# Loads of the next couples moved behind batch 0's block turns, and the next batch's z turned within a couple

## The chip, the cores and the metric

One core of one Trainium2 chip. The metric is the time on the device of one execution, in microseconds. Each comparison runs the kernel before and the changed one in turn on the same chip. The runs carry a state; ratios are the mean time of one kernel's fast runs over that of the other's fast runs of the same rounds, so they are not quite the ratio of the medians that I also quote. For a program on one core a run counts as slow when it is over 1.5% above the fastest of the same kernel. The kernel before spreads so widely (949 to 976 us over all calls) that this rule drops some of its longest runs; where it matters I say so. "Clock" is the clock that the chip granted to TensorE (the matmul engine) as a share of full speed; a "wait" is idle time of an engine before an instruction; a DMA "lands" when its data has arrived.

## The reference, cut to what matters

```
# u, v: (8, 3072, 256), z: (8, 3072, 64)
scores = (1.0 / S) * np.matmul(z, z.transpose(0, 2, 1))
attn = np.maximum(scores, 0.0) ** 2
x = (u * np.matmul(attn, v)).reshape(8 * 3072, 256)
return np.maximum(x @ w1, x @ w2) @ w_out
```

The scores are symmetric, so the kernel computes a block of 512 x 512 of the upper triangle once and gets its mirror by a transposing DMA, which I call a block turn.

## The kernel before

A batch has 6 groups of 512 rows; two groups are a couple. Batch 0 runs its first four groups in a plain stage, then its last couple; batches 1 to 7 run three couples each, and behind each couple a stage for the feed-forward part of the couple before. All turns (blocks, z and u) are issued in order by SyncE; all loads and stores by GpSimd, apart from batch 0's z, which SyncE loads.

```python
def mirror(b, g, blk):                      # a block turn: 128 x 2048 bf16, 512 KB
    t = Block(turned=True)
    nc.sync.dma_start_transpose(
        t.ap.rearrange("p (k r) -> p k r", r=P), A[b, g, blk].ap)
    ...
def load_z(b, piece, held=False):           # piece: a third of a batch's z
    zn[b, piece] = zpool.tile([P, 2 * G, dqk], bf16, name="zn")
    ...
    nc.gpsimd.dma_start(out=zn[b, piece], in_=...)      # fp32 to bf16
def turn_z(b, piece):
    t = zpool.tile([P, 2 * G, 2, dqk], bf16, name="zd")
    for h in range(2):
        nc.vector.tensor_copy(t[:, :, h, :], zn[b, piece])
    nc.sync.dma_start_transpose(zT[:, ds(z_at(b, piece * 2 * G), 2 * G), :], ...)
# ... load_v, load_u, turn_u alike
# plain stage, group i = 3:
if (i, n) == (3, 14):
    load_z(1, 2, held=True)
if (i, n) == (3, 18):
    load_v(1, 2, held=True)
if (i, n) in ((3, 12), (3, 20)):
    load_u(0, 4 + (n == 20))
# ...
# in a couple: at a step of TensorE an event can be run
for half, (name, w, blk, j) in enumerate(pair):
    ...
    if (s, half) in marks:                  # a half-done sum goes to the other half of the rows
        relay = nc.gpsimd.nop()             # TensorE waits for this relay some steps later
```

The relay matters below: GpSimd passes on a semaphore for TensorE between its own DMA issues, in program order.

## Time and profile before

| | kernel before |
|---|---|
| median, range | 965.23 us, 961.29 to 974.57 (3 runs) |
| TensorE busy | 910.9 of 961.9 us |
| longest waits of TensorE | 15.9 us for a block turn (once), 9.9 us for turns of z (five times) |
| DMA queues over the span | turns 60.7%, loads and stores 29.7% of 16 engines |

The lines, and what is read from them, are in the prediction.

### The profile page before, as it was taken

The page shows a single profiled execution, that of the slowest core. Times are in us where ns is not written, and L with a number is a line of the kernel's source. Part 1 is how long each engine was busy: PE and PEld are TensorE (multiplying, and loading weights), DVE is VectorE, ACT ScalarE, POOL GpSimd, SP SyncE. Part 2 cuts the span into 40 slices and gives each one's busy share as a digit, 9 for nine tenths or more (in the row PEclk, how much of TensorE's full clock was granted, in tenths as well). Part 3 has the DMA queues.
Part 4 walks back from the last instruction along what each step waited for, and adds up shares of the span by engine and source line. Part 5 has one row for each costly group of instructions (what it writes and reads, how often), then busy time and mean ns, then how long its engine had stood idle before and what let it go on. Part 6 is the DMA issues. An engine that isn't in the chain of part 4 may idle for free. (4 is left out here: it accounts for less than half of the span.)

```text
span 961.9 us, 19245 instructions
## 1 busy us (share of the span) xinstructions
PE 910.9 (95%) x7490; PEld 509.9 (53%) x7538; DVE 726.1 (75%) x1098; ACT 601.1 (62%) x1185; POOL 109.4 (11%) x207
## 2 busy tenths in 40 slices
PE   8994899999999999999999999999799999999995
PEld 3453454654655545555546545555365554555553
DVE  6770388796997789887997979978599788995620
ACT  6792677666675666666666666666566666664253
POOL 3110001101101101001111011011010110100000
PEclk9998899999999999999999999999999999999998
DMA  9999999999799997999989996989969899796211
GB/s 186 158 185 155 149 177 151 161 160 171 145 184 142 158 189 126 165 175 172 165 135 182 164 164 138 179 151 165 130 142 167 172 160 168 131 176 115 68 44 45
DMA packets 382509, 145.99 MB, mean 152 GB/s; under 512 B 361937, under 2 KB 365905, under 8 KB 382417
## 3 DMA queue, kind: packets, MB, share of 16 engines
q1 hardware_dynamic: 359328, 90.09, 60.7%
q0 software_dynamic: 23088, 54.67, 29.7%
q8 instruction: 59, 0.97, 0.4%
q14 instruction: 34, 0.27, 0.1%
HBM read 59.77 MB, written 25.17 MB: 88 GB/s over the span
## 5 line engine op out<-in xcount | busy, mean ns | idle before, releaser
L848 PE MATMUL acc<-blk,v_sb 64*128 64x512 bf16 x2208 | 454.4, 379 | 15.9 <-DMA blk<-blk 15.9
L221 ACT ACTIVATE r_sb<-s_ps 128x512 bf16<-128x512 f32 (+3 forms) x664 | 332.0, 556 | 148.6 <-PE s_ps L208 115.1
L848 PE MATMUL acc<-blk,vt 64*128 64x512 bf16 x1512 | 365.4, 377 | 0.0
L848 PEld LDWEIGHTS <-v_sb 64*128 64x128 bf16 x2208 | 180.3, 95 | 156.0 <-issue 23.5
L229 DVE TENSOR_TENSOR blk<-r_sb 128x1024 bf16<-128x1024 bf16 x251 | 168.8, 689 | 86.0 <-ACT r_sb L221 84.8
L454 PE MATMUL o_ps<-w_out_sb,g_sb 128*128 128x256 bf16 x1536 | 207.6, 273 | 7.3 <-ACT g_sb L438 5.0
L438 ACT ACTIVATE g_sb<-d_ps 128x512 bf16<-128x512 f32 x384 | 193.3, 630 | 27.6 <-PE acc L848 17.3
L848 PEld LDWEIGHTS <-vt 64*128 64x128 bf16 x1512 | 139.6, 94 | 62.6
L454 PEld LDWEIGHTS <-g_sb 128*128 128x128 bf16 x1536 | 150.0, 98 | 37.8 <-ACT g_sb L438 19.3
L431 PE MATMUL d_ps<-xT,w_sb 128*128 128x512 bf16 x720 | 167.5, 379 | 2.6 <-issue 0.2
L462 ACT COPY o_sb<-o_ps 128x512 f32<-128x512 f32 x96 | 56.2, 585 | 154.3 <-PE o_ps L454 111.9
L208 PE MATMUL s_ps<-zT 64*128 64x512 bf16 (+3 forms) x672 | 128.7, 359 | 10.8 <-DMA zT<-zd 9.9
L752 DVE TENSOR_TENSOR h_sb<-h_sb,acc 128x512 f32<-128x512 f32 x168 | 109.5, 683 | 28.4 <-ACT h_sb L756 18.6
L431 PEld LDWEIGHTS <-w_sb 128*128 128x128 bf16 x768 | 73.2, 98 | 89.6 <-issue 9.8
L463 POOL DMA_DIRECT2D out_dram<-o_sb x96 | 52.3, 545 | 562.2 <-ACT o_sb L462 562.2
L227 DVE TENSOR_TENSOR blk<-r_sb 128x512 bf16<-128x512 bf16 (+3 forms) x170 | 49.0, 323 | 56.9 <-ACT r_sb L221 55.8
L767 DVE TENSOR_TENSOR blk<-blk,blk 128x2048 bf16<-128x2048 bf16 x63 | 76.7, 1219 | 10.4 <-PE acc L848 10.4
L325 DVE TENSOR_TENSOR blk<-blk,blk 128x2048 bf16<-128x2048 bf16 x63 | 76.8, 1219 | 4.8 <-DMA blk<-blk 4.8
L329 DVE TENSOR_TENSOR blk<-blk,blk 128x2048 bf16<-128x2048 bf16 x63 | 77.2, 1225 | 2.1
L446 PE MATMUL o_ps<-W2o_sb,xT 128*128 128x256 bf16 x384 | 73.3, 273 | 0.0
L333 DVE TENSOR_TENSOR blk<-blk,blk 128x2048 bf16<-128x2048 bf16 x63 | 73.3, 1219 | 0.0
L208 PEld LDWEIGHTS <-zT 64*128 64x128 bf16 x672 | 36.9, 94 | 50.8 <-DMA zT<-zd 12.9
(51 smaller groups left out, 329.5 us busy)
## 6 DMA issues: line engine op xcount, KB each, us to landing
out_dram<-o_sb POOLq DMA_DIRECT2D x96, 256.0 KB, 3.1
un<-in_u_dram POOLq DMA_DIRECT2D x48, 256.0 KB, 6.7
v_sb<-in_v_dram POOLq DMA_DIRECT2D x21, 512.0 KB, 7.2
blk<-blk SPq DMA_TRANSPOSE x246, 5.7
zn<-in_z_dram POOLq DMA_DIRECT2D x21, 128.0 KB, 4.2
v_sb<-in_v_dram POOLq DMA_DIRECT2D x6, 256.0 KB, 8.0
blk<-in_moe_w_dram POOLq DMA_DIRECT2D x2, 512.0 KB, 6.4
uT<-un SPq DMA_TRANSPOSE x48, 4.8
```

Source lines behind the costliest of these rows:

```text
L208: nc.tensor.matmul(s_ps[h][:, lo[h] :], zT[rows, z_at(b, blk * G + tiles[h]), :], zT[rows, q + lo[h] // P : q + G, :].rearrange("p t c -> ...
L221: nc.scalar.activation(o, s, AF.Relu)
L229: nc.vector.tensor_mul(a[:, k : k + 2, :], r, r)
L325: nc.vector.tensor_add(*alike(f["S1"], f["A21"], f["A22"]))
L329: nc.vector.tensor_sub(*alike(f["S2"], f["S1"], f["A11"]))
L333: nc.vector.tensor_sub(*alike(f["S3"], f["A11"], f["A21"]))
L431: nc.tensor.matmul(d_ps, w15_sb[:, kc, ts(nb, P)], xT[:, kc, :], start=(kc == 0), stop=(kc == KD - 1),)
L438: nc.scalar.activation(g_sb[:, nb, :], d_ps, AF.Relu)
L454: nc.tensor.matmul(o_ps[:, t, :], g_sb[:, nb, ts(t0 + t, P)], w_out_sb[:, nb, :], start=False, stop=(nb == KF - 1),)
L752: nc.vector.tensor_add(out, a, b_)
L767: nc.vector.tensor_sub(f["A12"].ap, f["A12"].ap, f["S2"].ap)
L848: mm = nc.tensor.matmul(a.out(acc[name]), w()[rows], a.moving(rows, j), start=name not in opened, stop=left[name] == 0,)
```

## The change

It means to leave the DMA queues to the block turns while these have a backlog, and to have z turned long before the scores want it.

```diff
@@ plain stage, group 3
-                if (i, n) == (3, 14):
-                    load_z(1, 2, held=True)
-                if (i, n) == (3, 18):
-                    load_v(1, 2, held=True)
-                if (i, n) in ((3, 12), (3, 20)):
-                    load_u(0, 4 + (n == 20))
@@
-        second(PLAIN // 2 - 2, tasks + [lambda: turn_z(1, 2)])
+        second(PLAIN // 2 - 2, tasks)
@@ events of couple c of batch b (before: z loaded at 20, 30 and 20)
+                        (8, load_z, b + 1, 0),
+                        (14, load_z, b + 1, 1),
+                        (44, turn_z, b + 1, 0),
+                        (58, turn_z, b + 1, 1),
+                    ],
+                    [(8, load_z, b + 1, 2), (44, turn_z, b + 1, 2), (45, load_v, b + 1, 2)],
+                    [(10, load_v, b + 1, 1)],
@@ batch 0's last couple
+            if not b:
+                plan = [
+                    (2, load_z, 1, 2),
+                    (10, load_v, 1, 2),
+                    (20, turn_z, 1, 2),
+                    (24, load_u, 0, 4),
+                    (28, load_u, 0, 5),
+                    (40, load_v, 1, 1),
+                    (60, turn_u, 0, 4),
+                    (66, turn_u, 0, 5),
+                    (80, load_u, 1, 0),
+                    (88, load_u, 1, 1),
+                ]
@@ the stage behind a couple
-                if b and b + 1 < B and c < 2:
-                    tasks += [
-                        lambda piece=piece: turn_z(b + 1, piece) for piece in ((0, 1), (2,))[c]
-                    ]
```

(Cut: the same events written as a list instead of lambdas.)

More of the change, by code (lines that the diff above doesn't have):

```diff
@@ L808 @@
                 events[len(steps)] = [after_plain]
-            for n, do in (
-                (1, lambda: turn_u(b, q1)),
-                (4, lambda: turn_u(b, q2)),
-            ):
-                events.setdefault(n, []).append(do)
-            if i + 1 < len(couples):
-                later_b, later_c = couples[i + 1]
-                for n, g in ((36, 2 * later_c), (44, 2 * later_c + 1)):
-                    events.setdefault(n, []).append(lambda g=g: load_u(later_b, g))
-            for n, do in ():
-                events.setdefault(n, []).append(do)
-            if b + 1 < B:
-                for n, do in (
-                    ((20, lambda: load_z(b + 1, 0)), (30, lambda: load_z(b + 1, 1))),
-                    ((20, lambda: load_z(b + 1, 2)), (45, lambda: load_v(b + 1, 2))),
-                    ((10, lambda: load_v(b + 1, 1)),),
-                )[c]:
-                    if b or c == 2:
-                        events.setdefault(n, []).append(do)
+            plan = [(1, turn_u, b, q1), (4, turn_u, b, q2)]
+            if i + 1 < len(couples):
+                nb, nc_ = couples[i + 1]
+                plan += [(36, load_u, nb, 2 * nc_), (44, load_u, nb, 2 * nc_ + 1)]
+            if b + 1 < B:
+                plan += (
+                    [
+                        (8, load_z, b + 1, 0),
[5 more added lines that the diff above has]
+                    [(10, load_v, b + 1, 1)],
+                )[c]
+            if not b:
[11 more added lines that the diff above has]
+                ]
+            for n, do, *what in plan:
+                events.setdefault(n, []).append(lambda do=do, what=what: do(*what))
             asked = 0
```

## The prediction

> **What bounds the kernel now.** I read the page first, then the list of waits of TensorE, then the timeline around its longest wait, then the DMA queues of two stretches before that wait, and last the windows with their clocks.
>
> ```profile
> span 961.9 us, 19245 instructions
> PE 910.9 (95%) x7490; PEld 509.9 (53%) x7538; DVE 726.1 (75%) x1098; ACT 601.1 (62%) x1185; POOL 109.4 (11%) x207
> PE   8994899999999999999999999999799999999995
> PEclk9998899999999999999999999999999999999998
> ```
>
> TensorE is the bound: 910.9 of 961.9 us busy. About 51 us of the span is idle time of TensorE, and only that, with work done at a reduced clock, can be won without removing matmuls. The slices show two holes: slices 3 and 4 (digits 4 and 8) and slice 28 (digit 7). The list of waits of TensorE names them (engine, tile and line, what it waited for: us in total, times, longest):
>
> ```profile
> PE acc L848 <- DMA blk<-blk: 15.9, 1, 15.9
> PE s_ps L208 <- DMA zT<-zd: 9.9, 5, 5.2
> PE o_ps L454 <- ACT g_sb L438: 5.0, 28, 0.2
> ```
>
> One wait of 15.9 us is for a turned score block; five waits of 9.9 us in sum are for a turned z. Next the timeline of the issuing queues (SPq issues the turns, POOL the loads) and of TensorE:
>
> ```profile
> 50.22 0.54 POOL L180 DMA_DIRECT2D un<-in_u_dram  x1
> 57.78 34.75 SPq L257 DMA_TRANSPOSE blk<-blk  x7
> 65.09 0.53 POOL L132 DMA_DIRECT2D zn<-in_z_dram  x1 [14.33 <-DVE zn L131]
> 66.54 0.53 POOL L154 DMA_DIRECT2D v_sb<-in_v_dram  x1 [0.92 <-DVE v_sb L153]
> 67.06 0.54 POOL L180 DMA_DIRECT2D un<-in_u_dram  x1
> 92.64 2.73 SPq L140 DMA_TRANSPOSE zT<-zd  x1
> 95.47 4.52 SPq L257 DMA_TRANSPOSE blk<-blk  x2
> 99.98 1.01 PE L848 MATMUL acc<-blk,v_sb 64*128 64x512 bf16 x3 [15.88 <-DMA blk<-blk]
> ```
>
> Batch 0's last couple starts at 83.7 us and stops after one matmul: its first pair of steps needs block (5,4), the turned (4,5), and that is the last of batch 0's 15 turns in the queue. It was issued at 95.47 and landed at 99.94. From the trace's semaphore times and the program's wait values, what that turn reads was written by 63 us and its destination was free by 43; none of the turns issued from 57.8 to 97.6 waited for data. The queue itself was late. The DMA queues for 56 to 68 us, then for 68 to 86 us (packets, MB, share of 16 engines):
>
> ```profile
> q1 hardware_dynamic: 9355, 2.35, 115.5%
> q0 software_dynamic: 17, 0.02, 4.4%
> ```
> ```profile
> q1 hardware_dynamic: 2583, 0.65, 87.6%
> q0 software_dynamic: 501, 1.18, 39.7%
> ```
>
> Alone, the turns (q1) moved 2.35 MB in 12 us. Beside the loads of z, v and u (q0) they moved 0.65 MB in 18 us. A turn's packet took 1.155 x 16 x 12 us / 9355 = 24 ns in the first stretch and 0.876 x 16 x 18 us / 2583 = 98 ns in the second. One block landed every 2.4 us from 63.0 to 68.0; the next took 22 us. The windows add the clock (stretch, its length, busy us of PE, PEld, DVE, ACT, POOL with counts, then granted clock, DMA share, GB/s):
>
> ```profile
> 86.00:100.00 14.00, 0.02 (x2) 0.02 (x3) 0.00 (x0) 1.17 (x2) 1.08 (x2) 0.53 1.07 226
> 100.00:104.00 4.00, 4.00 (x22) 2.29 (x23) 1.26 (x4) 1.54 (x4) 0.00 (x0) 0.52 1.10 210
> 679.00:684.20 5.20, 0.07 (x2) 0.00 (x0) 1.22 (x2) 0.48 (x1) 0.00 (x0) 0.99 1.02 140
> 684.20:687.60 3.40, 3.38 (x18) 1.22 (x20) 1.46 (x2) 1.08 (x2) 1.07 (x2) 0.51 1.19 243
> ```
>
> After both long idle stretches TensorE works about 3.4 to 4 us at half clock.
>
> **What the Trainium skill says.** "DMA: Bandwidth & Descriptors", section "Issuing engines are not separate DMA queues", says that DMAs issued by sync and by gpsimd end on the same 16 DMA engines and interleave. The 24 against 98 ns agree. The same page, "Queues, rings and completion order", says that an engine goes round its queue rows a packet at a time. The trace has packets of 256 bytes for turns and of 1 to 4 KB for loads, so a turn should lose more than an equal share; 0.65 MB of turns against 1.18 MB of the others agrees in direction. "TensorE: Matmul & The Clock Gate", section "What's actually happening", gives half clock after an idle window of about 3.4 us and full clock after about as long of sustained work. The trace agrees: half clock to 103.86 after the first wait and to 687.54 after the one of 5.2 us.
>
> **The change, part by part.**
>
> (a) Removed from the plain stage: u of group 4 (issued 50.22), z piece 2 (65.09), v piece 2 (66.54) and u of group 5 (67.06), 256 + 128 + 512 + 256 = 1152 KB as landed. The turns keep their program order up to the one needed and the next. Without the loads, after the landing at 67.99 there remain four blocks, one z turn and the needed block. At 2.4 us a block and half for z that is 5.5 x 2.4 = 13.2 us: landing at 81.2. Group 4's load at 50.22 went beside a turn whose issue took 4.2 us against about 2.1 undisturbed, so the queue should be about 2 us earlier still: 79. Two stores (74.3 and 76.5) stay beside them; in 88 to 94 us two such stores cost about 1 us. So I expect landing near 80 to 82, before the 83.7 when it is needed. Gain: 15.9 us.
>
> (b) No idle stretch, no half clock: 99.98 to 103.86 at half costs 3.88 / 2 = 1.9 us. Gain 1.9.
>
> (c) z of the next batch. All five waits for zT fall in the third couple of a batch and are for piece 2, which before is turned at the end of the stage behind the second couple. Its turn is issued as the third couple starts, beside the load of v and two stores; in four of the five cases it took 8.6 to 14.3 us to land (4.4 is the median of all z turns), in the fifth it landed in 3.3 but was issued 7.6 us into the couple, behind a block turn. The change turns it at step 44 of the second couple's 84, with its load at step 8. A couple of this kind takes 21 us and the stage behind it 16.3 (653.3 to 669.6), so the turn is issued about 10 + 16 = 26 us earlier, and even 14.3 us to landing is covered. Gain 9.9 us (0.6 + 1.5 + 1.5 + 5.2 + 1.2), and at 684.22 to 687.54 another 3.3 / 2 = 1.7 us of half clock. The count of copies and turns stays, so VectorE has the same work in other places (two copies of 286 ns each).
>
> (d) Added to batch 0's last couple: the 1152 KB, together with v of piece 1, which moves from step 10 to 40. The loads of u for batch 1 move to steps 80 and 88. The first of these waits for the turn of group 4's u, and GpSimd also relays half-done matmuls in this couple; the last relays that TensorE waits for are at steps 83 and 87, wanted at 88 and 92. The couple takes 26.8 - 1.9 = 24.9 us for 96 steps, so step 80 is at +20.7 and step 88 at +22.8. Group 4's load is issued at +6 and should land by +13 to +16 (in this couple's traffic of before, v took 7.2 us, u 6.0 and 8.2); its turn follows in 5 to 8 us. It is just in time. Likewise z piece 2 is loaded at step 2, turned at step 20 (+5.2) and wanted by scores at step 58 (+15.1): with 4.4 us median and 10 us under load it fits, without much room. For these two I give back 2.5 us.
>
> Sum: 15.9 + 1.9 + 9.9 + 1.7 - 2.5 = 26.9 us. From the median of 965.2: 938.3 us. I say 938.
>
> **Rivals.** First, the stall moves: the loads collide with the turns inside the last couple, the z or u turns land 10 to 16 us after issue, and TensorE waits 3 to 8 us there or at the start of batch 1. For it: loads of v and u beside turns made a landing of 22 us once. Against it: that was with a backlog of turns, while in this couple the turns are held back by their own data and landings stayed under 10 us before. Time then 942 to 948. Second, the slow stretch from 68 to 86 is not due to the loads: from 76 to 82 us q0 moved little, yet turns stayed slow, and two stores were in flight. Then the needed block lands late all the same, perhaps half the wait stays, and the time is about 947. Against it: v and u were still unfinished until 81.7 and 83.3, and two stores at 88 to 91 left the turns near their pace. Third, z turns inside a couple delay the mirrored blocks behind them on the in-order queue, and VectorE waits: 2 to 4 us. Against it: VectorE waited for blocks only 4.8 us in all, and it is 75% busy.
>
> **Range and chances.** With everything won and nothing given back it is 965.2 - 29.4 = 936; a quicker before run takes some us off this (its three runs lie 961.3 to 974.6). With the first or second rival it is 942 to 951. So 931 to 951 holds it 8 times in 10. Two per cent is 945.9, a gain of 19.3: it needs all of (a), (b) and a little, or half of (a) with all of (c). Faster 0.84, same 0.15, slower 0.01.
>
> **What would show it.** The waits of TensorE: the one for blk<-blk gone or under 2 us, those for zT<-zd gone; clock at 1.00 from 80 to 110 and near 684 minus the gain. The needed block's turn landing before 84 and turns at about 24 ns a packet from 56 to 80. A new line of waits for zT or for GpSimd between 84 and 110 us would be rival one; a block wait of 5 us or more with no loads beside it, rival two. I am wrong if the stalls vanish and the span does not fall with them.

## The result, and the profile after

The changed kernel took 939.57 us (936.79 to 942.12, 4 runs) beside 969.32 us (961.29 to 974.57) of the kernel before: ratio 0.970, interval 0.962 to 0.978. The page of the changed kernel, its span and two rows of the 40 slices:

```profile
span 939.1 us, 19291 instructions
PE   9999889999999999999999999999999999999995
PEclk9999999999999999999999999999999999999998
```

Slices are counted from 0. Slices 3 and 28, at 4 and 7 before, are at 9. Slice 4 is at 8 as before, and slice 5 went from 9 to 8: there the new waits lie. TensorE's waits from batch 0's last couple on (engine, tile and line, what it waited for: us in total, times, longest; those of 0.2 us and less are left out):

```profile
PE acc L853 <- POOLq L862: 2.1, 1, 2.1
PE acc L853 <- DVE blk L329: 1.6, 1, 1.6
PE s_ps L208 <- ACT o_sb L462: 1.2, 1, 1.2
PE s_ps L208 <- DMA zT<-zd: 0.6, 1, 0.6
```

No wait for a block turn is left, and of 9.9 us for turned z only 0.6, in another place. Four small new waits, 5.5 us in sum, all lie between 98 and 133 us. The queue of turns in the changed kernel, where the needed block is the first of the two turns in the second line:

```profile
72.89 1.79 SPq L140 DMA_TRANSPOSE zT<-zd  x1
74.78 6.96 SPq L257 DMA_TRANSPOSE blk<-blk  x2
```

It was issued at 74.78 in place of 95.47 and landed at 81.88. The last couple began at 83.0, 1.1 us later, and did not wait. The DMA queues of 68 to 86 us, to compare with the same stretch in the prediction (q1 holds the turns, q0 the loads and stores; packets, MB, share):

```profile
q1 hardware_dynamic: 10865, 2.73, 93.8%
q0 software_dynamic: 320, 1.05, 17.9%
```

The turns moved 2.73 MB in these 18 us in place of 0.65. A packet of a turn took 0.938 x 16 x 18 us / 10865 = 25 ns in place of 98. The 1.05 MB of q0 are mostly the four stores. Two of them (73.59 and 75.77) ran beside the turns up to the needed one. These turns landed 6.5 to 7.1 us after issue, where the four before them took 4.6 to 4.7, and from 73 to 82 us turns and stores together moved 205 GB/s, beside 214 for turns alone from 68 to 72.9 us. So two stores beside turns cost a few us, and are not what made the slow stretch. The windows of the changed kernel (length, busy us of PE, PEld, DVE, ACT, POOL, then granted clock, DMA share, GB/s):

```profile
86.00:100.00 14.00, 13.37 (x126) 6.14 (x124) 7.11 (x14) 11.23 (x22) 1.96 (x4) 1.00 1.04 141
128.80:132.20 3.40, 1.22 (x10) 0.41 (x7) 3.33 (x4) 0.65 (x2) 0.54 (x1) 1.00 1.26 139
132.20:135.70 3.50, 2.92 (x15) 1.16 (x16) 3.50 (x4) 2.49 (x5) 1.08 (x2) 0.51 1.23 286
```

Where TensorE stood idle before (86 to 100), it works at full clock. After the waits of 1.6 and 1.2 us the clock was at half from 132.25 to 135.66 us, and TensorE was busy for 2.9 us of that.

The sum over the two traces: 15.9 + 1.9 + 9.9 + 1.7 = 29.4 us went, 5.5 us of waits and 2.9 / 2 = 1.4 us of half clock came, which leaves 22.5; the spans differ by 961.9 - 939.1 = 22.8. The medians of the timed runs differ by more, 29.7. That is the first sign that one trace of the kernel before is not all of it.

### The profile page after: what moved, and what is told of

It reads as the page before. It is cut to its first block, busy times and chain, and to the rows that moved or that the text cites. A ratio compares the mean times of both kernels' runs of the same rounds, so it can differ in the third digit from the quotient of the medians.

```text
span 939.1 us, 19291 instructions
## 1 busy us (share of the span) xinstructions
PE 912.3 (97%) x7538; PEld 516.2 (55%) x7538; DVE 722.4 (77%) x1096; ACT 599.0 (64%) x1185; POOL 110.2 (12%) x207
## 5 line engine op out<-in xcount | busy, mean ns | idle before, releaser
L853 PEld LDWEIGHTS <-v_sb 64*128 64x128 bf16 x2208 | 176.7, 94 | 138.0 <-issue 9.8
L431 PE MATMUL d_ps<-xT,w_sb 128*128 128x512 bf16 x768 | 173.9, 379 | 0.0
L746 DVE TENSOR_TENSOR h_sb<-h_sb,acc 128x512 f32<-128x512 f32 x168 | 109.5, 683 | 26.5 <-ACT h_sb L750 18.8
L415 DVE SCALAR_TENSOR_TENSOR xT<-h_sb,uT 128x512 bf16<-128x512 f32 x96 | 59.9, 684 | 0.0
```

The source lines that it names most:

```text
L431: nc.tensor.matmul(d_ps, w15_sb[:, kc, ts(nb, P)], xT[:, kc, :], start=(kc == 0), stop=(kc == KD - 1),)
L746: nc.vector.tensor_add(out, a, b_)
L853: mm = nc.tensor.matmul(a.out(acc[name]), w()[rows], a.moving(rows, j), start=name not in opened, stop=left[name] == 0,)
```

## The experiments

Twelve runs were made, in three calls of four; some repeat a kernel without an edit. I tell them by question.

### Do the two parts add? (z_only, b0_only)

The first is the kernel before with the z part only:

```diff
-                    ((20, lambda: load_z(b + 1, 0)), (30, lambda: load_z(b + 1, 1))),
-                    ((20, lambda: load_z(b + 1, 2)), (45, lambda: load_v(b + 1, 2))),
+                    loads of z at 8, 14 and 8, turns at 44, 58 and 44; v at 45
-                if b and b + 1 < B and c < 2:
-                    tasks += [... turn_z(b + 1, piece) ...]
```

(Cut: the added lines are told in words.)

> The kernel before with only the z part of the change (batches 1 to 7: z loaded at steps 8 and 14, turned at steps 44 and 58 of a couple; batch 0 as before). My theory: the two parts add, this one is worth the five waits for zT, 9.9 us, and the 1.7 us of half clock near 684 us. So about 957 to 958 in the rounds where before is 969, ratio 0.988; the wait of 15.9 us for blk stays, the waits for zT in the third couples are gone. Rival (delayed mirrors on the in-order queue): the zT waits go but waits of VectorE for blocks grow by 2 to 4 us and TensorE gets new waits; ratio 0.992 or more.

The second is the changed kernel with that part undone, so only batch 0 is changed.

> The changed kernel with only the batch 0 part (z of batches 2 to 7 loaded and turned where the kernel before does). My theory: the wait for blk gone (15.9), its half clock gone (1.9), and the three new waits of the changed kernel stay (zT 0.6, GpSimd relay 2.1, VectorE 1.6 with 1.2 and 1.7 of half clock): net about 17.8 - 7.2 = 10.6, ratio 0.989, with four or five zT waits of about 10 us in sum still there. Rival: if the parts help each other (fewer turns late everywhere), the zT waits shrink too and the ratio is under 0.98.

Measured: z_only 942.17 us, ratio 0.987 (0.980 to 0.994). b0_only 955.88 us, ratio 1.000 (0.995 to 1.006), beside a kernel before at 958.92 (948.72 to 973.39, 11 runs). In the trace of z_only the waits for zT are gone and the one for the block stays:

```profile
PE acc L857 <- DMA blk<-blk: 15.2, 1, 15.2
```

In that of b0_only it is the other way round; one of the four waits (3.8 us) is in batch 0's last couple, the other three (11.4 us) in third couples later:

```profile
PE s_ps L208 <- DMA zT<-zd: 15.2, 4, 5.3
```

So each part takes away the wait it is meant for. In z_only VectorE waited 4.6 us for blocks, 4.8 before, and TensorE not at all through it: the rival of delayed mirrors falls. The z part's size (1.3% of 959 is 12.5 us; the interval allows 6 to 20) agrees with the 11.6 that was predicted. The batch 0 part alone gained nothing that these runs resolve, where 10.6 us had been expected. Here the rule on states matters, since it drops four of the 11 runs before; over all runs the means are 960.4 and 956.2 us. But z_only has something odd: its recorded first run took 950.97 us at a clock of 0.988, and its other three 937.66 to 943.57 at 0.993 to 0.994. A wait of 15 us brings 17 us of half clock with it, which is 0.9% of the mean clock, so those three runs are unlikely to have had it in full.

### Is the long wait there in every execution? (before_again, z_only_again)

Both are repeats without an edit, for a second trace and more runs.

> The kernel before a second time, for a second trace of it: is the wait of 15.9 us for blk the same each time, and which of the third couples wait for zT? My first theory (fixed sizes): blk wait 14 to 17 us with about 17 us of half clock, zT waits of about 10 us in sum. The rival, which the timed runs of the kernel with only the z part suggest (clocks of 0.993 to 0.994, where 17 us of half clock would give 0.986): the long blk wait is there only in some executions, mostly in those whose DMA packets are recorded; then the trace shows about 15 again, but timed runs of the kernel with only the z part stay near 941.

> The kernel before with only the z part, more rounds. If the blk wait is in every execution, timed runs lie near 949 with a clock near 0.988. If it is only in recorded ones, the first run lies near 950 with a clock of 0.988 and the timed ones near 941 with 0.993 or more, and the batch 0 part is worth next to nothing on top of the z part in timed runs.

Measured: before_again 962.75 us, ratio 1.000 (0.992 to 1.009). z_only_again 947.53 us (942.83 to 956.45), ratio 0.989 (0.982 to 0.995). The waits in the second trace of the kernel before (this execution counts as slow; I use it for the waits' sizes alone, not for a time):

```profile
PE s_ps L208 <- DMA zT<-zd: 19.2, 6, 8.4
PE acc L848 <- DMA blk<-blk: 7.0, 1, 7.0
```

and in the second trace of z_only, which is of state fast:

```profile
PE acc L857 <- DMA blk<-blk: 6.5, 1, 6.5
```

The rival was half right. The long wait is not in every execution; but it is not tied to recording either, because these two recorded executions have 7.0 and 6.5 us. Timed runs of z_only_again reach 950 to 956 with clocks of 0.986 to 0.990, which fits the long wait, though no trace shows it for them. The same program, with the same loads at the same times, has two outcomes: in the short one v piece 2 (512 KB) landed 7.8 and 8.3 us after its issue, in the long one 15.2 and 15.5, and the first turn beside it in 9.8 and 10.5 against 22.0 and 20.5. From 66 to 82 us all queues together moved 212 and 190 GB/s in the two short traces, near the 214 of turns alone, and 102 and 111 in the two long ones. So in the short outcome the loads cost about the time of their bytes; in the long one turns and loads both slow down. Of z_only's ten runs four were over 950 us and six under 946.

### Which load does it? (v_back, v_moved)

v_back is the changed kernel with v piece 2 alone in the plain stage again:

```diff
+                if (i, n) == (3, 18):
+                    load_v(1, 2, held=True)
-                    (10, load_v, 1, 2),
```

> The changed kernel with v piece 2 alone (512 KB) loaded in the plain stage again, held as before; z and u stay in batch 0's last couple. Theory now: a large load beside the backlog of block turns slows both, for 8 us of v's landing in a good execution and 15 in a bad one, and a blk wait of 7 or 15 to 17 us follows. v is the largest of the loads, so most of the wait comes back: blk wait of 4 us or more, v landing in 8 us or more. Rival: it takes v and u together; then v lands in under 7 us and the blk wait is under 2 us.

v_moved is the kernel before with v piece 2 alone moved out of it (step 10 of the last couple, v piece 1 at 40).

> The kernel before with v piece 2 alone taken out of the plain stage (to step 10 of batch 0's last couple, v piece 1 to step 40); z piece 2 and both u stay. If v is the main cause the blk wait is between 2 and 5 us (the 640 KB that stay cost 3.3 us in part in the kernel with z alone in the plain stage); if z and u suffice for the slow stretch it is 7 us or more.

Measured, one run each (state unknown): 938.67 and 959.02 us. The trace of v_back:

```profile
PE acc L854 <- DMA blk<-blk: 3.4, 1, 3.4
```

The trace of v_moved:

```profile
PE s_ps L208 <- DMA zT<-zd: 16.3, 5, 5.1
PE acc L846 <- DMA blk<-blk: 3.0, 1, 3.0
```

v alone (512 KB) costs 3.4 us, the other 640 KB alone 3.0; all together cost 6.5 to 17.5 (five traces: 15.9, 15.2, 7.0, 6.5, and 17.5 in v_late below). In v_back v landed in 7.1 us. That v is the main cause is not shown: v_back came out just under its "4 us or more" (the rival's "under 2" fails too), and v_moved, whose 3.0 lies in the 2 to 5 expected for that case, kept nearly as much of the wait without v. Nor does the wait go by size: z_early below has 3.3 us with the 128 KB of z alone. The long outcome was only seen with all the loads together; single looks cannot say that it never comes with one of them.

These looks also differ in something that the edits don't touch. In every trace a load of z and one of u start at 35 to 37 us beside two block turns, which land 9.4 to 14.8 us after issue. The next turn was issued at 45.4 us in the third trace of the changed kernel and at 50.3 in z_early. So part of a wait of about 3 us can come from how late the queue already was; v_behind_z below, with none of the moved loads there, still waited 0.9 us.

### Why was the z turn late? (v_late)

The kernel before with one number changed:

```diff
-                    ((10, lambda: load_v(b + 1, 1)),),
+                    ((45 if b else 10, lambda: load_v(b + 1, 1)),),
```

> The kernel before with one number changed: in the third couples of batches 1 to 6 the load of v piece 1 goes from step 10 to step 45. It tells why the late z turn is slow. Theory of collision: without the 512 KB beside it the z turn issued at the couple's start lands in 3 to 6 us, before the scores want it at about +9.5 us, so the zT waits are gone or under 1 us in sum, and the time is within 3 us of the kernel with only the z part. Rival, that it is late because it is issued late and the two stores and turns of u alone fill the engines: the waits stay at 5 us or more in sum.

Measured: 958.06 us, ratio 1.001 (0.992 to 1.009). Its recorded run took 991.78 us and is of state slow, so I take waits and landings from it, and no time:

```profile
PE acc L848 <- DMA v_sb<-in_v_dram: 24.5, 2, 14.4
PE acc L848 <- DMA blk<-blk: 17.5, 1, 17.5
PE acc L848 <- DVE blk L329: 3.8, 4, 1.6
```

No wait for zT stands in the list. The turns of piece 2 landed 4.0 to 6.6 us after issue in every batch (8.6 to 14.3 us in five of six batches of the first trace before, 3.3 in the other). The collision with v is what made the z turn slow: that half of the theory holds. The half about the time fails (within 3 us of z_only was expected): v piece 1, now issued about 9 us ahead of the next couple's v piece 0, collided with it. Piece 0 landed up to 32.4 us after issue in this trace, and TensorE waited for it in two of the batches. The collision moved instead of going away.

### Can the new waits be taken away? (u_behind_v, z_early, v_behind_z, with after_again and after_third)

u_behind_v takes the two loads of u for batch 1 out of steps 80 and 88 and issues them behind v piece 0, so that GpSimd does not stand still with a relay behind it:

```diff
-                    (80, load_u, 1, 0),
-                    (88, load_u, 1, 1),
 ...
                 load_v(b + 1, 0)
+                if not b:
+                    load_u(1, 0)
+                    load_u(1, 1)
```

> The changed kernel with the two loads of u for batch 1 issued behind that of v piece 0, after batch 0's last couple, in place of steps 80 and 88 in it. My theory: GpSimd's wait for the turn of u held the relay (2.1 us) and then held back v piece 0, whose late landing (126.5) made VectorE wait 5.5 us and TensorE 1.6 + 1.2, and half clock 1.7. So v piece 0 issues at about 109 and lands by 118, those four terms vanish: 6 us faster than the changed kernel, about 933, and no wait for POOLq. Rival: the slow stretch is made by two stores and two block turns beside the load, whenever it starts: the relay wait goes (2.1) but VectorE still waits for v and the time is about 937.

> The changed kernel once more on the same chip, as the yardstick for the kernel with u behind v: ratio to before about 0.970 (0.962 to 0.978), the same three new waits at the same places: zT near 98.5, POOLq near 108.8, VectorE L329 near 130.8 us.

Measured on one chip: u_behind_v 939.46 us, ratio 0.984 (0.979 to 0.988); the changed kernel again 940.53 us, ratio 0.985 (0.978 to 0.991), outside the 0.962 to 0.978 that I expected. No difference between the two, where my theory had 6 us. The wait for GpSimd is not in u_behind_v's trace, as both theories said, but its list has this:

```profile
PE s_ps L208 <- DMA zT<-zd: 4.2, 1, 4.2
```

That is z piece 2, turned at step 20 beside v piece 2 and both u, landing 13.0 us after issue. The second trace of the changed kernel has the same wait at 2.9 us and neither the one for GpSimd nor that for VectorE, so of its "same three waits" one came. The new waits vary as the old ones do.

z_early therefore loads and turns z piece 2 (128 KB) in the plain stage as the kernel before does, in addition to u behind v:

```diff
+                if (i, n) == (3, 14):
+                    load_z(1, 2, held=True)
-                    (2, load_z, 1, 2),
-                    (20, turn_z, 1, 2),
-        second(PLAIN // 2 - 2, tasks)
+        second(PLAIN // 2 - 2, tasks + [lambda: turn_z(1, 2)])
```

> The changed kernel with the two loads of u for batch 1 behind v piece 0, and with z piece 2 loaded and turned in the plain stage as the kernel before does; v and u stay in batch 0's last couple. Theory: the wait for zT at step 58 (0.6 to 4.2 us and up to 1.7 of half clock in three traces) goes, no wait for GpSimd, and z's 128 KB in the plain stage delay the block turns by under 1 us: about 936, 4 us faster than the changed kernel. Rival: a single load beside the backlog of turns is enough to start the slow stretch: a blk wait of 5 us or more comes back and the time is 945.

Measured: 940.39 us, ratio 0.980 (0.975 to 0.984). The zT wait went and one of 3.3 us for the block came:

```profile
PE acc L851 <- DMA blk<-blk: 3.3, 1, 3.3
```

Neither the 936 of the theory nor the 945 of the rival came. Not shown to be faster than the changed kernel: 940.39 here, 940.53 there on another chip.

v_behind_z goes the other way. It keeps z in the couple and moves the large loads behind its turn (on top of u behind v):

```diff
-                    (10, load_v, 1, 2),
-                    (24, load_u, 0, 4),
-                    (28, load_u, 0, 5),
-                    (40, load_v, 1, 1),
+                    v piece 2 at 26, u at 30 and 34, v piece 1 at 52
```

(Cut: the added lines are told in words; u behind v as above.)

> The changed kernel with u of batch 1 behind v piece 0 as in the earlier run, and in batch 0's last couple v piece 2 at step 26, u of groups 4 and 5 at 30 and 34, v piece 1 at 52, so that z piece 2 is turned at step 20 with no large load beside it. Theory of collision: z's turn lands in under 6 us, no wait for zT at step 58, no blk wait, no wait for GpSimd: a trace with no wait of TensorE over 1 us from 60 us on and about 934 to 936 recorded, 2 to 5 us under the changed kernel in timed runs. Rival: the loads only move the collision on, to the u turns and v piece 0, and VectorE's combines make TensorE wait 2 to 5 us at the start of batch 1.

> The changed kernel on the same chip as the one with v behind z, as its yardstick, and a third trace: zT wait of 0.6 to 4 us at step 58 of batch 0's last couple, no blk wait over 1 us, no zT wait in batches 1 to 7; ratio to before 0.97 to 0.985.

Measured on one chip: v_behind_z 952.75 us (949.55 to 954.61), ratio 0.993 (0.988 to 0.999); the changed kernel 940.73 us, ratio 0.981 (0.975 to 0.988). The waits of v_behind_z (cut: one of 1.2 us for GpSimd at 687 us, and one of 0.5):

```profile
PE acc L851 <- DVE vt L170: 13.2, 1, 13.2
PE acc L851 <- DMA blk<-blk: 0.9, 1, 0.9
PE acc L851 <- DMA v_sb<-in_v_dram: 0.5, 1, 0.5
```

and its DMA issues from 92 to 127 us (KB each, median us to landing):

```profile
v_sb<-in_v_dram POOLq DMA_DIRECT2D x2, 512.0 KB, 18.3
blk<-blk SPq DMA_TRANSPOSE x5, 12.4
```

z's turn landed in 4.7 us as planned, and no wait for zT is left. But four loads, 1.5 MB, now start within 7.3 us (91.05 to 98.36), two loads of v need 18.3 us each, and the turns of u come late: the first, issued at 103.98, took 22.4 us, and the second was issued only at 126.22 and landed at 131.33. VectorE's program has the product with u ahead of the combine of v piece 0, and it stood still for both:

```profile
DVE xT L415 <- DMA uT<-un: 19.1, 2, 15.4
```

v piece 0 had landed at 126.26, but its combine was not through before 139.8, and TensorE waited 13.2 us. The rival, which named the u turns, was right and its 2 to 5 us were too small. All six runs lie above all six of the changed kernel, by 12 us in the median, so as far as times tell the long outcome came every time. The changed kernel's own four loads start within 8.2 us (85.82 to 94.06 in the first trace), and their two v landed in 7.8 and 8.5, 7.3 and 10.1, 6.3 and 7.2 us in its three traces. So the margin is narrow, and what tips a group of loads from one outcome to the other is not settled by these runs.

The third trace of the changed kernel lacks the wait for zT that I expected (0.6 to 4 us), and has no wait over 1 us from 60 us on but this:

```profile
PE acc L853 <- DVE blk L329: 1.1, 1, 1.1
```

No version here is shown to beat the changed kernel.

One sum ties all traces together. Take from the span of each the waits of TensorE over 0.5 us and half of its busy time at half clock, both from 60 to 900 us. What remains is 931.4 to 933.8 us in all fourteen traces, those of slow runs among them. So these waits, with the half clock behind them, are what separates the executions; to within 2.4 us no other cause is needed. By the same count the block wait with its half clock cost 17.8, 9.0, 17.2 and 8.2 us (before twice, z_only twice), and the late z turns of batches 1 to 7 cost 11.6, 27.1, 18.8 and 21.0 (before twice, b0_only, v_moved). b0_only also lost 6.7 us in batch 0's last couple. That fits its ratio of 1.000: it takes away 8 to 18 us, gives back 6.7, and the z turns that stay vary by 15.

## Why the prediction was right, point by point

The predicted 938 us met 939.57, inside the range, and "faster" came out in the first call. In the two repeats the gain is not clear of 2%. The waits named were the right ones; that the sizes added up so well is partly luck, as told below. By its steps:

- **(a) The needed block would land at 80 to 82, and the wait of 15.9 us would go.** Mechanism shown: it landed at 81.88, turns kept 25 ns a packet, and the wait is in none of the three traces of the changed kernel. Of its corrections, the queue was 2.4 us earlier (2 expected), and the two stores cost about 3 us (1 expected). The size was off as a forecast of the usual execution: 15.9 was the long outcome. The other traces with the same batch 0 have 15.2, 17.5, 7.0 and 6.5 us.
- **(b) 1.9 us of half clock would go.** Shown: clock 1.00 from 86 to 104 us in the first trace. The second has a new stretch at half clock there, behind a wait for zT, counted under (d).
- **(c) The waits for zT would go, 9.9 + 1.7 us.** Shown in z_only and in every trace of the changed kernel for batches 1 to 7. The ratios of z_only, 0.987 and 0.989, are 12.5 and 11 us of 959 and 962, close to the 11.6. The traces say more: with half clock the late z turns cost 11.6, 27.1, 18.8 and 21.0 us, so the trace that the prediction read had the least of them. It also had the long outcome of (a). A large (a) and a small (c) offset each other in the sum; that is the luck. v_late shows the reason given, the collision with v.
- **(d) 2.5 us given back in batch 0's last couple.** Both places named there did cost: 0.6 us for z at step 58, 2.1 us for GpSimd's wait for the turn of u. The third cost, VectorE late at the start of batch 1 behind a slow load of v piece 0, fits the place that the first rival names, not its path. The three traces' waits are 5.5, 2.9 and 1.1 us, with half clock 6.9, 4.6 and 1.1; so 2.5 was somewhat low.
- **Rivals.** The first (the stall moves) came true in small; in v_behind_z it came true in full. The second (not the loads but the stores) falls by the changed kernel's 68 to 86 us: 1.05 MB of q0, two stores among the turns in question, and turns at 25 ns. The third (delayed mirrors) was not seen.
- **What the steps did not see.** They took one trace as the kernel before. Its median in later calls was 958.92, 961.64 and 963.65, and the ratio of the changed kernel 0.985 and 0.981 where it had been 0.970. Part of that is the rule on states, which dropped no run before in the first call and four of 11 in each of these two; the means of all runs give 0.980 and 0.975. The batch 0 part, 15.3 us net in my sum, gained nothing resolvable alone (ratio 1.000), and the changed kernel is 2 to 7 us below z_only (940.5 against 942.2 on one chip, and 947.5 on another), which is not resolved either. That this part takes its wait away is shown; what it is worth in time is not. The forecast of 938 held because the changed kernel itself is steady: 940.53 and 940.73 in the other two calls.

## What to carry to other kernels

When a wait is caused by transfers colliding, trace the same kernel more than once before sizing it: here the same wait was 7 or 16 us. Then check the sum: span less waits and half clock should be the same in every trace. Spread large loads that run beside transposing DMAs, and check where they land after a move: moving loads closer together brought the same slow stretch back elsewhere, 12 us worse. A turn that is needed early in a stage is best issued a stage ahead, which here won 11 to 12 us in the mean of fast runs, with no new wait over 1.2 us in its two traces.

## What the Trainium skill lacked or had wrong

- "DMA: Bandwidth & Descriptors", "Issuing engines are not separate DMA queues", says that DMAs of all issuers share 16 engines and interleave. It doesn't say that loads beside transposing DMAs can cost both far more than the time of their bytes: a turn's packet went from 24 to 98 ns, all queues together fell from 214 GB/s to 102, v's 512 KB landed in 7.8 us or in 15.2 for the same program, and in up to 32.4 us in v_late. No page gives a rule for when.
- The same page, "Latency and other measured facts", gives 261 GB/s, measured on one kernel, for a DMA transpose with a middle dimension that is not contiguous. There is no one figure here: undisturbed block turns mostly landed every 2.4 us, 524288 bytes / 2.4 us = 218 GB/s, but from 61.2 to 63.6 us of the changed kernel they moved 277 GB/s. The runs don't show why.
- "TensorE: Matmul & The Clock Gate", "What's actually happening", ties half clock to an idle window of about 3.4 us. In the changed kernel two waits of 1.6 and 1.2 us with matmuls between them, 1.22 us busy in a window of 3.4 us, were followed by 3.4 us at half clock. In its second trace a lone wait of 2.9 us, from 98.44 to 101.30, was followed by half clock from 102.45 to 105.86; a lone wait of 1.1 us in its third trace was not, nor one of 3.3 us in z_early. So a window need not be wholly idle, and the length of a wait alone does not decide.
